# Input loads further ahead, and the first early job written after the eighth unit, in a gated scan with routed experts

## The chip, the core and the metric

The kernel runs on one core of one Trainium2 chip. The metric is the device time of an execution in microseconds (us). The engines are PE (TensorE, the matrix engine), DVE (VectorE), ACT (ScalarE), POOL (GpSimd) and SP (SyncE, which here only issues DMAs and reads registers). In the profile "PEld" is PE's loading of weights, "SPq" and "ACTq" are DMA issues by SP and ACT, and "Lnnn" is a line of the kernel.

## What is computed

A gated recurrence along the sequence feeds a two-level mixture of experts, in which every token goes to one of 16 experts:

```python
sig = 1.0 / (1.0 + np.exp(-f_logit))              # x, f_logit: 4 x 3648 x 256
f = lower_bound + (1.0 - lower_bound) * sig
h[t] = f[t] * h[t - 1] + (1 - f[t]) * x[t]        # for every batch row, start 0
# x is now h, 14592 tokens of 256
g = argmax(x @ w_group)                           # one of 4 groups
e = argmax(x @ w_expert[g])                       # one of 4 experts of the group
out[token] = softmax_g * softmax_e * (relu(x @ w1[g, e]) @ w2[g, e])   # 256 -> 1024 -> 256
```

## The kernel before, in words

**Units.** The 14592 tokens are worked through as 29 units of 512, numbered from 0 (so the eighth unit is unit 7). Unit u goes through these steps. `p1_load` (L167) brings 1 MB of inputs into one of four `zt` buffers; units up to 11 are loaded from SP's queue, later ones from ACT's. ACT computes the gate by Tanh and an affine step (`p1_tanh`, `p1_affine`, L185 to L203). DVE multiplies the input by the gate (L218 or L238) and runs one scan for each half of the 256 channels (`p1_tb`, L229). The scan of a unit starts from the last column of the unit before it. PE multiplies the result with the router's weights (`p1_router`, L275) and turns the answer over (`p1_logits`, L288). PE also turns the scan's result back into rows of tokens (`p1_back`, L256), which ACT copies out. For a group of one or two units (`GROUPS`) the routing follows: DVE finds the largest logits, PE counts the tokens of every expert (L380 to L383, "run-offs"), DVE computes each token's place, and POOL scatters the rows by indirect DMA into the lists `xs` in DRAM (L358), 128 rows at a time.

**Early jobs.** A list long enough is worked on before all units are done. `EARLY` gives 16 jobs as (unit, tiles of 128 tokens): jobs 0 and 1 at units 5 and 6, jobs 2 and 3 at unit 8, 4 and 5 at unit 10, and so on. At its unit, `pick` (L573) chooses on DVE the fullest list; SP reads the choice into a register (L589), and writes blank rows below the list's end (L592). Then come the weights of the job (`job_weights`, L841 to L849, asked for by `fetch_to`), the load of its rows `xr` (`job_rows`, L831), which waits for the scatters of all units ahead of its own, the transposes of these rows (`job_xt`, L912), and the two products with ReLU between (`m1_step`, `m2_step`). Jobs 0 and 1 are "raw": they multiply in fp32 (L943, L978) with no splitting of weights, with 22 matmuls for warming (`keep_warm`, L265) ahead of the transposes. The other jobs use split weights, three products each (L965 to L967, L995). After the units, 16 further jobs work off what is left of the lists.

**Order.** SP issues everything in the order in which the program is written. PE, DVE and ACT are held to the written order only inside the block at L1128 to L1131; what is written behind that block is placed by the scheduler, which may also move it ahead into gaps it sees. Inside the block stands all of the background program up to the mark of the first row load (`start_macro(0)` runs it up to `marks[5]`), and then job 0's weights and `job_xt`. The background program is a list of small functions made by `p1_thunks` (L404). Up to unit 9 (`FAST`) the part for unit u begins with the load of unit u + 2, then, by `ROWS_AT`, the row load of job 0 (at u = 6) or job 1 (at u = 7), and only then the gate of the next unit, the router of unit u - 1, the scans, the routing, and `pick`. `pick` ends with `fetch_to`, which asks for four pieces of weights. So before, job 0's transposes are written ahead of all the rest of unit 6. Behind the block, the jobs' products and the background program are interleaved by due times.

Of the kernel before, what the change touches and what calls it, by code (L numbers as in the profile page):

```python
# [36 lines left out]
O_BUFS = 5  # L37
X_BUFS = 4
AHEAD = 3
MT = -(-max(CAPS) // 128)  # L40
QUARTERS = (13, 14, 15)
ZX_SP = 12
# [3 lines left out]
def gated_scan_moe(ctx: ExitStack, tc, zx, lower, wroute, wexp, out, S):  # L46
# [118 lines left out]
    last_load = {}  # L165

    def p1_load(u):  # L167
        if u >= NU:
            return
        a, b = unit_range(u)  # L170
        w = b - a
        zt = p1.tile([P, 2, KD, UNIT], F32, name="zt", bufs=4)
        src = zx[u * P:(u + 1) * P, :].rearrange("p (s k w) -> p s k w", s=2, k=KD)
        if u == 0:
            for k in range(KD):
                for q in range(2):
                    nc.sync.dma_start(out=zt[:, q, k, 0:w], in_=src[:, q, k, 0:w])
        elif u == 1:
            for k in range(KD):
                nc.sync.dma_start(out=zt[:, :, k, 0:w], in_=src[:, :, k, 0:w])  # L180
        else:
            last_load[u] = (nc.sync if u < ZX_SP else nc.scalar).dma_start(out=zt[:, :, :, 0:w], in_=src[:, :, :, 0:w])
        units[u] = {"z": zt}
# [220 lines left out]
    def p1_thunks(us, groups, parts):  # L404
# [36 lines left out]
        def wave(u, n):  # L441
            while parts and n and parts[0][0] <= u:
                put(parts.pop(0)[1])
                n -= 1
# [13 lines left out]
        for u in us + [us[-1] + 1]:  # L458
            seq = []
            if u <= FAST:  # L460
                put(lambda u=u: p1_load(u + AHEAD - 1))
                for m in [m for m, v in ROWS_AT.items() if u == v]:
                    f = lambda m=m: early_rows(m)
                    f.mark = m
                    put(f)
                ending = u - 1 in ends
                if not ending:
                    put(lambda u=u: p1_ta(u + 1))
                if u > 0:
                    put(lambda u=u: p1_router(u - 1))  # L470
                    put(lambda u=u: logits(u - 1))
                    if u > 1:
                        put(lambda u=u: p1_gate(u))
                put(lambda u=u: p1_tb(u, 0))
                wave(u, 1)
                if ending:
                    bind, bound, (s1, f4x, s2, f3, f4, s6, f5, s7s) = routing(u - 1)
                    put(bind)
                    put(lambda u=u: p1_tanh(u + 1))
                    put(s1)  # L480
                    put(f4x)
                    if u > 1 and member[u - 2] == member[u - 1]:
                        back(u - 2)
                    put(s2)
                    put(f3)
                    put(f4)
                    wave(u, 1)
                    put(lambda u=u: p1_affine(u + 1))
                    back(u - 1)
                    put(bound)  # L490
                    put(s6)
                    put(f5)
                    for f in s7s:
                        put(f)
                    wave(u, 1)
                elif u > 7:
                    wave(u, 1)
                    back(u - 1)
                if u in cuts and u - 1 in ends:
                    put(lambda u=u: pick(u))  # L500
                put(lambda u=u: p1_tb(u, 1))
                wave(u, 1 if u < FAST else 99)
                if u == FAST:
                    f = lambda: None
                    f.mark = "begun"
                    put(f)
                    for v in [v for v in sorted(cuts) if v <= FAST and v not in ROWS_AT]:
                        f = lambda v=v: early_rows(v)
                        f.mark = v
                        put(f)  # L510
                continue
            if u in us:
                seq += [lambda u=u: (p1_load(u + AHEAD - 1), u + 1 in us and p1_ta(u + 1))]
            if u - 1 in us:
                seq += [lambda u=u: p1_back(u - 1, 0)]
            if u in us:
                seq += [lambda u=u: p1_tb(u, 0)]
            if u - 1 in us:
                seq += [lambda u=u: p1_router(u - 1)]
                seq += [lambda u=u: p1_back(u - 1, 1)]  # L520
            if u in us:
                seq += [lambda u=u: p1_tb(u, 1)]
            if u - 1 in us:
                seq += [lambda u=u: logits(u - 1)]
            for t in seq:
                put(t)
                slot += 1
                for _ in range(1):
                    if not hold:
                        break  # L530
                    f = hold.popleft()
                    if isinstance(f, tuple):
                        lagq.append((slot + LAG, f[1]))
                    else:
                        put(f)
                while lagq and lagq[0][0] <= slot:
                    put(lagq.popleft()[1])
            if u - 1 in ends:
                grp = ends[u - 1]
                T = sum(unit_range(v)[1] - unit_range(v)[0] for v in grp) // P  # L540
                G = {}

                def bind(G=G, first=grp[0]):
                    G.update(cur.pop("G"))
                    G["rows"] = group_rows.pop(first)
                if u <= 13:
                    s1, f4x, s2, f3, f4, s6, f5, s7s = route_thunks(G, T, True)
                    rs = [s1, s2, f3, f4x, None, f4, f5, s6] + s7s
                else:
                    rs = route_thunks(G, T)  # L550
                    rs[3:3] = [None] * 2
                put(bind)
                if u in cuts:
                    rs.append(lambda u=u: pick(u))
                    f = lambda u=u: early_rows(u)
                    f.mark = u
                    rs.append(("lag", f))
                hold.extend(rs)
# [14 lines left out]
    def pick(u):  # L573
# [24 lines left out]
        V.scalar_tensor_tensor(out=got, in0=pos, scalar=float(n * P), in1=eoff, op0=ALU.add, op1=ALU.subtract)  # L598
        V.tensor_tensor(out=got, in0=got, in1=sel, op=ALU.mult)
        V.tensor_tensor(out=taken, in0=taken, in1=got, op=ALU.add)  # L600
        fetch_to(pptr[0] + 4)

    asked = set()

# [255 lines left out]
    def job_xt(j, pi):  # L860
# [58 lines left out]
        else:  # L919
            hi = j.xh[ch][:, :, c0:c0 + rows]  # L920
            nc.scalar.copy(hi, tpv)
            nc.vector.tensor_tensor(out=j.xl[ch][:, :, c0:c0 + rows], in0=tpv, in1=hi, op=ALU.subtract)  # L922
        meta = mo.tile([P, 2, 2], I32, name="meta", bufs=16)
        tc.keep_in_program_order(nc.vector.tensor_copy(meta[:, 0:m], r[:, 0:m, D:D + 2]))
        if j.kind != "A":
# [201 lines left out]

    with tc.manual_schedule(engines={mybir.EngineType.PE, mybir.EngineType.DVE, mybir.EngineType.Activation}):  # L1128
        start_macro(len(PLAN))
        for t in prep_thunks(macros[len(PLAN)][0]):  # L1130
            t()  # L1131
    pending = None
# [92 lines left out]
```

## Time and profile before

| | us |
|---|---|
| median of 3 runs (lowest to highest) | 802.14 (800.18 to 803.07) |
| the profiled execution | 802.48 |
| its span in the trace | 800.7 |

Of the span PE is busy for 91%, DVE for 67%, ACT for 57% and POOL for 36%. The chip moves 152.02 MB by DMA, 189 GB/s over the span. The page shows the span in 40 slices of 20 us: in the first eight PE is busy for 2, 7, 2, 9, 8, 6, 8 and 5 tenths, and its granted clock is 9, 8, 6, 7, 9, 8, 9 and 7 tenths of full speed; after that PE stays at 9 and the clock too. A busy PE is no PE at its peak, since matmuls are pipelined and a lower clock stretches them, so a stretch is read by its idle time and its clock together.

### The profile page before, as it was taken

How to read it: one execution, taken by the hardware profiler on the slowest of the kernel's cores; microseconds unless marked ns; L12 is line 12 of the kernel's file. 1: busy time of each engine (PE TensorE's matmuls, PEld its weight loads, DVE VectorE, ACT ScalarE, POOL GpSimd, SP SyncE). 2: the span in 40 equal slices, each digit the busy share in tenths (PEclk: the TensorE clock that was granted, in tenths of full speed). 3: DMA queues.
4: the chain of work that ended last, by engine and by line, in shares of the span. 5: the costliest groups of instructions: out<-in, count | busy, mean ns of one | idle time of the engine just before them, and what ended most of it. 6: DMA issues, size and time to landing. Idle time of an engine off the chain costs nothing.

```text
span 800.7 us, 21431 instructions
## 1 busy us (share of the span) xinstructions
PE 725.3 (91%) x8131; PEld 641.8 (80%) x8131; DVE 535.2 (67%) x1140; ACT 453.4 (57%) x820; POOL 289.0 (36%) x272
## 2 busy tenths in 40 slices
PE   2729868599999999899999999999999999999995
PEld 1527646388888888799989989898999999889995
DVE  6945459589999999469645573645545656556651
ACT  6715557478788786445555554444454555546652
POOL 3641416435666556553112211222222223223222
PEclk9867989799999999999999999999999999999999
DMA  7672989968888865665788654344333555556530
GB/s 273 229 229 69 336 303 275 330 226 285 289 308 296 263 220 181 207 190 153 226 178 197 163 151 92 117 99 118 116 106 126 143 158 166 160 157 180 167 81 28
DMA packets 101977, 152.02 MB, mean 190 GB/s; under 512 B 60975, under 2 KB 71000, under 8 KB 98544
## 3 DMA queue, kind: packets, MB, share of 16 engines
q1 hardware_dynamic: 87328, 103.27, 45.8%
q0 software_dynamic: 11424, 30.02, 10.4%
q10 hardware_dynamic: 3120, 17.34, 5.9%
q8 instruction: 64, 1.05, 0.6%
q14 instruction: 41, 0.34, 0.2%
HBM read 112.66 MB, written 38.38 MB: 189 GB/s over the span
## 4 chain that ended last, share of the span: by engine, by line
PE 61%; DVE 12%; DMA 9%; issue 5%; ACT 4%; POOL 1%; SPq 1%; POOLq 0%; DVEq 0%; ACTq 0%
PE ps_m L995 29%; PE ps_m L965 6%; PE ps_m L966 6%; PE ps_m L967 6%; DVE wl L858 3%; PE ps_p L965 3%; PE ps_p L966 3%; PE ps_p L967 3%; DVE hl L971 2%; DMA zt<-in_zx_dram 2%; DVE h L229 2%; DMA xr<-xs 2%; DMA xs<-rows,posi 2%; DMA xs<-blank 1%; PE ps_p L256 1%
## 5 line engine op out<-in xcount | busy, mean ns | idle before, releaser
L995 PE MATMUL ps_m<-wh,hl 128*128 128x256 f16 (+4 forms) x1256 | 254.9, 251 | 0.1
L995 PE MATMUL ps_m<-wh,hh 128*128 128x256 f16 (+4 forms) x1256 | 254.7, 252 | 0.0
L995 PE MATMUL ps_m<-wl,hh 128*128 128x256 bf16 (+4 forms) x1256 | 254.6, 251 | 0.0
L995 PEld LDWEIGHTS <-hh 128*128 128x128 f16 (+4 forms) x2512 | 186.8, 99 | 22.0 <-issue 3.3
L966 PE MATMUL ps_m<-xl,wh 128*128 128x256 bf16 (+10 forms) x790 | 192.5, 257 | 5.9 <-DVE xl L922 3.2
L965 PE MATMUL ps_m<-xh,wh 128*128 128x256 f16 (+10 forms) x790 | 192.3, 257 | 3.2 <-DVE hl L971 2.7
L967 PE MATMUL ps_m<-xh,wl 128*128 128x256 f16 (+10 forms) x790 | 192.5, 257 | 0.0
L358 POOL DMA_INDIRECT xs<-rows,posi x114 | 138.4, 1214 | 128.2 <-issue 29.0
L858 DVE TENSOR_TENSOR wl<-st,wh 128x1024 bf16<-128x1024 f32 x120 | 144.6, 1217 | 52.9 <-ACT wh L857 52.7
L1008 POOL DMA_INDIRECT out_dram<-o,info x71 | 82.6, 1164 | 237.3 <-ACT o L1007 214.6
L971 DVE SCALAR_TENSOR_TENSOR hl<-ps_m,hh 128x512 bf16<-128x512 f32 (+9 forms) x169 | 112.4, 671 | 70.6 <-ACT hh L970 65.3
L970 ACT ACTIVATE hh<-ps_m 128x512 f16<-128x512 f32 (+9 forms) x169 | 99.3, 589 | 61.7 <-PE ps_m L967 58.6
L857 ACT CAST wh<-st 128x1024 f16<-128x1024 f32 x120 | 123.9, 1047 | 17.6 <-DMA st<-in_wexp_dram 7.7
L967 PEld LDWEIGHTS <-wl 128*128 128x128 bf16 x1088 | 107.2, 99 | 13.5 <-issue 6.2
L966 PEld LDWEIGHTS <-wh 128*128 128x128 f16 x1088 | 107.3, 99 | 11.3 <-issue 3.9
L965 PEld LDWEIGHTS <-wh 128*128 128x128 f16 x1088 | 107.3, 99 | 10.3 <-issue 1.4
L1008 POOL DMA_INDIRECT out_dram<-o,meta x57 | 63.1, 1107 | 138.8 <-ACT o L1007 116.7
L995 PEld LDWEIGHTS <-hl 128*128 128x128 bf16 (+4 forms) x1256 | 99.6, 99 | 10.1 <-issue 0.4
L1007 ACT ACTIVATE o<-ps_m,info 128x256 f32<-128x256 f32 (+3 forms) x71 | 31.6, 446 | 72.1 <-PE ps_m L995 64.2
L965 PE MATMUL ps_p<-xh,wh 128*128 128x256 f16 (+14 forms) x298 | 70.8, 252 | 0.0
L966 PE MATMUL ps_p<-xl,wh 128*128 128x256 bf16 (+14 forms) x298 | 70.7, 251 | 0.0
L967 PE MATMUL ps_p<-xh,wl 128*128 128x256 f16 (+14 forms) x298 | 70.6, 251 | 0.0
(181 smaller groups left out, 828.4 us busy)
## 6 DMA issues: line engine op xcount, KB each, us to landing
st<-in_wexp_dram SPq DMA_DIRECT2D x120, 512.0 KB, 6.3
zt<-in_zx_dram ACTq DMA_DIRECT2D x16, 1024.0 KB, 8.6
zt<-in_zx_dram SPq DMA_DIRECT2D x10, 1024.0 KB, 6.0
xs<-blank SPq DMA_DIRECT2D x28, 258.0 KB, 4.9
xr<-xs SPq DMA_DIRECT2D x14, 258.0 KB, 2.9
wh<-in_wexp_dram SPq DMA_DIRECT2D x8, 256.0 KB, 7.1
wl<-in_wexp_dram SPq DMA_DIRECT2D x8, 256.0 KB, 6.6
xs<-rows,posi POOLq DMA_INDIRECT x114, 7.3
```

The source lines that it names most:

```text
L229: nc.vector.tensor_tensor_scan(out=h[:, k, c0 - a:c1 - a], data0=ff[:, k, c0 - a:c1 - a], data1=uu[:, k, c0 - a:c1 - a], initial=init, op0 ...
L358: sc = nc.gpsimd.indirect_dma_start(out=xs_v[G["t0"] + t][:, :], out_offset=bass.IndirectOffsetOnAxis(ap=R["posi"][:, t:t + 1], axis=0), i ...
L857: nc.scalar.copy(j.wh[i], j.st[i])
L858: nc.vector.tensor_tensor(out=j.wl[i], in0=j.st[i], in1=j.wh[i], op=ALU.subtract)
L965: nc.tensor.matmul(po, w1_at(j.wh, k, c), xh[:, k], start=(k == 0), stop=False)
L966: nc.tensor.matmul(po, w1_at(j.wh, k, c), xl[:, k], start=False, stop=False)
L967: nc.tensor.matmul(po, w1_at(j.wl, k, c), xh[:, k], start=False, stop=(k == KD - 1))
L970: nc.scalar.activation(hi, pv, AF.Relu)
L971: nc.vector.scalar_tensor_tensor(out=j.hl[ch][:, cs[0]:cs[-1] + 1, 0:w], in0=pv, scalar=0.0, in1=hi, op0=ALU.max, op1=ALU.subtract)
L995: nc.tensor.matmul(pm[i * q:i * q + n, 0:dw], h[ch][:, c, ts], w2_at(w, c)[:, i * dw:(i + 1) * dw], start=(c == 0 and s == 0), stop=(c == ...
L1007: nc.scalar.activation(o[s, 0:dw], pm[s, 0:dw], AF.Copy, scale=lt.bitcast(F32)[s, r, 1:2])
L1008: nc.gpsimd.indirect_dma_start(out=out_v[out_n[0]].rearrange("n (g d) -> (n g) d", g=g), out_offset=bass.IndirectOffsetOnAxis(ap=lt[s, r, ...
```

## The change

Five edits. (1) Up to unit 9, the part for unit u now asks for the loads up to unit u + 3 (`FAR`), where it asked for unit u + 2; a unit that is loaded already is skipped. The number of buffers stays four. (2) The row loads of jobs 0 and 1 move from the start of the parts for units 6 and 7 to just ahead of the second scan there, behind `pick` of unit 6. (3) The weights that `pick` asked for at its end are now asked for behind these row loads (and behind `pick` elsewhere). (4) A new mark stands behind the scans of unit 7 (`BEGIN`), and the block with the written order runs the background program up to it before job 0's weights and transposes. (5) Raw jobs no longer copy token numbers and output weights out of the row tile, they read them from there.

```diff
--- before.py
+++ after.py
@@ -37,6 +37,8 @@
 O_BUFS = 5
 X_BUFS = 4
 AHEAD = 3
+FAR = 4
+BEGIN = 7
 MT = -(-max(CAPS) // 128)
 QUARTERS = (13, 14, 15)
 ZX_SP = 12
@@ -165,7 +167,7 @@
     last_load = {}
 
     def p1_load(u):
-        if u >= NU:
+        if u >= NU or u in units:
             return
         a, b = unit_range(u)
         w = b - a
@@ -458,11 +460,7 @@
         for u in us + [us[-1] + 1]:
             seq = []
             if u <= FAST:
-                put(lambda u=u: p1_load(u + AHEAD - 1))
-                for m in [m for m, v in ROWS_AT.items() if u == v]:
-                    f = lambda m=m: early_rows(m)
-                    f.mark = m
-                    put(f)
+                put(lambda u=u: [p1_load(v) for v in range(u + AHEAD - 1, u + FAR)])
                 ending = u - 1 in ends
                 if not ending:
                     put(lambda u=u: p1_ta(u + 1))
@@ -498,8 +496,18 @@
                     back(u - 1)
                 if u in cuts and u - 1 in ends:
                     put(lambda u=u: pick(u))
+                for m in [m for m, v in ROWS_AT.items() if u == v]:
+                    f = lambda m=m: early_rows(m)
+                    f.mark = m
+                    put(f)
+                if u in cuts and u - 1 in ends:
+                    put(lambda: fetch_to(pptr[0] + 4))
                 put(lambda u=u: p1_tb(u, 1))
                 wave(u, 1 if u < FAST else 99)
+                if u == BEGIN:
+                    f = lambda: None
+                    f.mark = "first"
+                    put(f)
                 if u == FAST:
                     f = lambda: None
                     f.mark = "begun"
@@ -551,7 +559,7 @@
                     rs[3:3] = [None] * 2
                 put(bind)
                 if u in cuts:
-                    rs.append(lambda u=u: pick(u))
+                    rs.append(lambda u=u: (pick(u), fetch_to(pptr[0] + 4)))
                     f = lambda u=u: early_rows(u)
                     f.mark = u
                     rs.append(("lag", f))
@@ -598,7 +606,6 @@
         V.scalar_tensor_tensor(out=got, in0=pos, scalar=float(n * P), in1=eoff, op0=ALU.add, op1=ALU.subtract)
         V.tensor_tensor(out=got, in0=got, in1=sel, op=ALU.mult)
         V.tensor_tensor(out=taken, in0=taken, in1=got, op=ALU.add)
-        fetch_to(pptr[0] + 4)
 
     asked = set()
 
@@ -920,6 +927,9 @@
             hi = j.xh[ch][:, :, c0:c0 + rows]
             nc.scalar.copy(hi, tpv)
             nc.vector.tensor_tensor(out=j.xl[ch][:, :, c0:c0 + rows], in0=tpv, in1=hi, op=ALU.subtract)
+        if j.raw:
+            j.meta.append(r[:, 0:m, D:D + 2])
+            return
         meta = mo.tile([P, 2, 2], I32, name="meta", bufs=16)
         tc.keep_in_program_order(nc.vector.tensor_copy(meta[:, 0:m], r[:, 0:m, D:D + 2]))
         if j.kind != "A":
@@ -1127,6 +1137,7 @@
 
     with tc.manual_schedule(engines={mybir.EngineType.PE, mybir.EngineType.DVE, mybir.EngineType.Activation}):
         start_macro(len(PLAN))
+        bg_to(marks["first"])
         for t in prep_thunks(macros[len(PLAN)][0]):
             t()
     pending = None
```

## Rows read from the trace of the kernel before

**Rows 1.** Page, first part: engine busy us, share of span, instructions.

```profile
PE 725.3 (91%) x8131; PEld 641.8 (80%) x8131; DVE 535.2 (67%) x1140; ACT 453.4 (57%) x820; POOL 289.0 (36%) x272
```

**Rows 2.** Stretches: length, busy of PE, PEld, DVE, ACT, POOL; clock, DMA share, GB/s.

```profile
45.60:60.70 15.10, 0.00 (x0) 0.03 (x1) 4.85 (x6) 0.48 (x1) 3.88 (x3) 0.63 0.87 270
60.70:70.00 9.30, 9.30 (x43) 6.43 (x43) 4.83 (x12) 4.55 (x11) 0.00 (x0) 0.50 0.00 0
85.70:88.60 2.90, 0.18 (x1) 0.01 (x1) 0.00 (x0) 0.43 (x1) 0.21 (x1) 1.00 0.98 362
105.10:112.30 7.20, 0.64 (x4) 0.25 (x2) 0.67 (x1) 4.23 (x6) 0.00 (x0) 0.91 0.81 303
144.30:153.50 9.20, 0.00 (x0) 0.00 (x0) 7.46 (x8) 6.51 (x10) 7.04 (x6) 0.73 1.03 402
200.00:315.00 115.00, 113.08 (x1168) 99.76 (x1165) 113.84 (x245) 91.41 (x173) 73.14 (x57) 1.00 0.80 268
350.00:792.00 442.00, 439.23 (x5437) 401.98 (x5436) 258.17 (x480) 226.87 (x383) 115.83 (x103) 1.00 0.54 146
```

**Rows 3.** Timeline, 59 to 90 us: start, us, engine, line, idle before and releaser.

```profile
60.22 1.06 ACT L192 ACTIVATE zt<-zt 128x1024 f32<-128x1024 f32 x1 [17.66 <-DMA zt<-in_zx_dram]
...
60.70 0.47 PE L912 MATMUL ps_p<-ident,xr 128*128 128x128 f32 x1 [15.12 <-DMA xr<-xs]
...
61.01 0.17 DVE L924 COPY meta<-xr 128x4 int32<-128x4 int32 x1 [10.53 <-DMA xr<-xs]
...
89.48 0.32 DVE L330 TENSOR_REDUCE sm<-ex 128x40 f32<-128x160 f32 x1 [10.92 <-ACT ex L388]
```

**Rows 4.** Timeline of SP's DMA issues, 0 to 100 us.

```profile
4.66 24.35 SPq L182 DMA_DIRECT2D zt<-in_zx_dram  x6
...
50.96 0.34 SPq L182 DMA_DIRECT2D zt<-in_zx_dram  x1
...
73.19 0.36 SPq L592 DMA_DIRECT2D xs<-blank  x1
...
79.33 0.34 SPq L182 DMA_DIRECT2D zt<-in_zx_dram  x1
...
92.84 0.79 SPq L182 DMA_DIRECT2D zt<-in_zx_dram  x1
```

**Rows 5.** Stretches, columns as in rows 2.

```profile
33.80:45.45 11.65, 9.57 (x109) 8.15 (x107) 10.76 (x31) 7.94 (x18) 9.07 (x9) 0.77 0.36 129
60.70:72.00 11.30, 11.30 (x79) 7.72 (x79) 6.68 (x24) 5.72 (x15) 0.12 (x1) 0.59 0.00 0
72.00:153.50 81.50, 56.88 (x397) 44.40 (x393) 55.36 (x121) 50.39 (x95) 37.57 (x32) 0.91 0.91 306
```

**Rows 6.** Chain of waits in order of time: start, us, what.

```profile
49.12 7.22 DMA xs<-rows,posi
56.58 3.98 DMA xr<-xs
...
133.03 8.52 DMA xs<-rows,posi
141.56 11.86 DMA xr<-xs
```

**Rows 7.** Groups on PE, 60.7 to 79.4: count, busy us, mean ns, idle before.

```profile
L256 PE MATMUL ps_p<-ident,h 128*128 128x128 f32 x24 | 4.5, 328 | 0.0
L275 PE MATMUL ps_p<-h,wr 128*32 128x128 f32 x64 | 3.6, 314 | 0.0
...
L380 PE MATMUL ps_p<-runoff,row 1*128 1x80 f32 (+1 forms) x4 | 1.2, 395 | 0.0
L288 PE MATMUL ps_p<-ident,rs 128*128 128x128 f32 x3 | 1.0, 332 | 0.0
```

**Rows 8.** Timeline of DVE, 30 to 52 us: second scan of unit 4; of unit 7.

```profile
33.78 1.27 DVE L229 TENSOR_TENSOR_SCAN h<-zt,h 128x512 f32<-128x512 f32 x1
...
49.41 1.07 DVE L229 TENSOR_TENSOR_SCAN h<-zt 128x448 f32<-128x448 f32 x1
```

## The prediction

> **What bounds the kernel now.** I read the engine shares first. PE (TensorE) is busy for 725.3 us of 800.7 [rows 1], so the end moves only if PE waits less or does its early work at the higher clock. The table of stretches says where it waits. From 350 to 792 us PE is busy for 439.23 of 442 us, and from 200 to 315 us for 113.08 of 115, while DVE (VectorE) is busy for 113.84 there [rows 2]. Neither stretch has anything to give, and both need rows and units delivered earlier if they are to end earlier. The idle time lies ahead of them: 15.1 us (45.6 to 60.7), 2.7 us (85.7 to 88.6), 6.6 us (105.1 to 112.3) and 9.2 us (144.3 to 153.5) [rows 2]. Then the waits and the chain say who ended these. At 60.70 PE had waited 15.12 us for the rows of job 0. ACT had then waited 17.66 us for the input of unit 8. DVE's next long stop, 10.92 us at 89.48, ends with an exponential on ACT, which itself stood behind the Tanh of unit 9 [rows 3]. That input was asked for only at 79.33, because SP issues in written order and the load stood behind job 1's choice, blank rows and eight weight loads, which began at 73.19 [rows 4]. The choice was late because it needs the routing of unit 5, whose PE work stood behind job 0's transposes. So one blocked instruction at 45.6 made three later waits. While it lasted, transfers dried up too: from 60.7 to 72.0 the DMA share is 0.00, and from 72.0 to 153.5 it is 0.91 [rows 5]. The second half of the early stage is paced by transfers whose first 11.3 us were given away.
>
> **Part by part.**
>
> *Job 0's program after unit 7.* In the block with a written order, units 6 and 7 now come before job 0's 22 warming matmuls and four transposes. The rows of job 0 come no sooner: the last scatter they wait for starts at 49.12 and takes 7.22 us, the load 3.98 us [rows 6], so about 60.6. But in 45.6 to 60.7 PE ran nothing, and it can now do what it did for units 5 and 6 behind the rows. The groups after 60.7 give 3.6 us for the routers of four units (half, 1.8), 4.5 us for the back transposes of three (one of them falls before the mark, 1.5), 1.0 for the logits transposes of three (two, 0.7) and 1.2 for the run-off products of two routings (one, 0.6; with the counts behind it I take 1.0) [rows 7]. Sum 5.0 us off the path. The cover is DVE's: it must do unit 5's routing, the second choice and the scans of 6 and 7 by then. The scans of 6 and 7 ended by 50.8 [rows 8], and DVE was busy only 4.85 of the 15.1 us, so 10.2 us are free; the 9.3 us after 60.7, which hold unit 5's routing with a gate and a scan, took 4.83 us [rows 2]. With two waits for the run-off copy of some 1.5 us I put the mark at 56 to 61 us. If it slips past 60.6, each us costs one us, up to the 5.0 gained.
>
> *Loads three units ahead.* Loads up to 7 already go out the moment their buffer is free (six issues over 24.35 us [rows 4]); nothing is gained there. Load 8 needs the buffer of unit 4, whose second scan starts at 33.78 [rows 8]; it is now written ahead of the first choice and goes out near 35.1 in place of 50.96, into a stretch with a DMA share of 0.36 [rows 5]. Load 9 comes behind job 0's weights, at about 51 in place of 79.33. Load 10 comes behind job 1's weights, at about 62. Load 11 waits for unit 7's scans and stands behind job 1's rows: about 65 in place of 92.84 [rows 4]. So the ACT waits of 17.66 us and the DVE wait of 10.92 us [rows 3] should go, and with them the PE stops of 2.7 and 6.6 us [rows 2], since the second is ReLUs queued on ACT behind the input of units 11 and 12 and job 2's late rows. The new waits: on SP, loads 9 to 11 wait for scans of unit 5, 6 and 7, with row loads and weights queued behind; by the times above those scans are over when SP arrives, cost 0, at worst one pair of scans, about 2.5 us [rows 8]. Load 12 goes out from ACT right behind unit 8's scans. The trace of before has no such wait on ACT; between 0 and a gate with two scans (about 4 us) I take 1, because ACT's copies for routing stand ahead of it.
>
> *The second choice ahead of the first row load.* On SP the value load, 1 blank and then job 0's row load; only after that the eight weight loads of job 1 (some 0.7 us apiece, between the blank at 73.19 and the load at 79.33 [rows 4]). Job 0's row load is held by the scatters until 56.3 [rows 6] anyway, so a choice made by about 54 costs nothing; each us that the choice is later than 56.3 delays job 0's rows by as much. Before, the row load waited for no choice of unit 6. This and the mark have the same cover, and the same price.
>
> *Raw jobs take their offsets and weights out of the row tile.* Two DVE copies go (0.17 us each, nothing on the sum); the 10.53 us that DVE stood at the first one [rows 3] goes with the reordering. In return the row buffers of jobs 0 and 1 are held until their outputs are written. There are six; jobs 2 and 3 take one each, job 4 two, so job 5 would be the first to meet them, long after. Cost 0.
>
> **The sum.** From PE: 5.0 + 2.7 + 6.6 = 14.3 us, less 1 for load 12. From transfers, independently: the empty 11.3 us are refilled (job 1's weights, loads 10 and 11, unit 5's scatters), up to 3.5 us more from moving load 8 (1 MB at the 306 GB/s of the busy stretch) [rows 5]. Both describe the same shift of the early stage and are not added. I take 12 us. The 9.2 us before 153.5 stay: their chain is scatter 8.52, then row load 11.86 us [rows 6], and nothing in the change shortens it; it only begins sooner. The clock I leave out: PE ran 60.7 to 70.0 at a granted 0.50 (1.2 GHz) [rows 2] after 15 idle us, which cost 4.65 us; with PE partly occupied before, some may come back. The profiled execution took 802.5 us, hence 790.5; the median of the runs is 0.3 below it, hence 790. After 160 us PE and DVE are both full, so the shift is handed on whole.
>
> **Rivals.** *Only the reordering counts (about 797).* If SP's queue keeps loads 9 to 11 about where they were, the 5.0 us of PE work remain: 802.1 - 5. For it: SP must still wait for the choice and for scatters of unit 5. Against it: load 9 stands ahead of both.
>
> *Given back at the row loads (about 802).* From 72 us on transfers run at 0.91 [rows 5]. If jobs 2 to 5 get their rows when they do now because the scatters of units 6 to 9 are no earlier, PE, having done jobs 0 and 1 sooner, waits longer at 105 and 144. For it: 402 GB/s just before 153.5 [rows 2], at which nothing more fits. Against it: those scatters followed on DVE stops that should vanish.
>
> *Slower: the early loads crowd job 0's rows (about 807).* Job 0's scatters and row load are alone on the path. A row load took 3.98 us here and 11.86 us at 141.56, where much else was in flight; the scatters before them 7.22 and 8.52 us [rows 6]. With loads 8 to 10 and two jobs' weights beside them, job 0 could get its rows 7.9 + 1.3 = 9.2 us later, 69.8. PE has 5.0 us of earlier work to set against it, so the kernel loses 4.2 us if the later waits return too: 802.5 + 4.2 = 806.7. It decides from a landing later than 65.6. Against it: in 45.6 to 60.7 the share was already 0.87 [rows 2], and load 8 has left that stretch.
>
> The Trainium skill (DMA: Bandwidth & Descriptors, section Queues, rings and completion order) speaks for this rival: every one of the sixteen engines takes its queue rows in turn, packet by packet, so loads from SP and scatters from POOL slow each other whoever issued first. By that rule alone, a scatter and row load each sharing evenly would double, 11.2 us more, which would make it about 809; the row at 133.03, 8.52 us in a crowded stretch, does not bear out a doubling of the scatter.
>
> **How the numbers follow.** Forecast (a gain of 8 to 20 us): 0.55. Only the reordering: 0.15. Given back: 0.15. Slower: 0.15. Less than 0.5% (4 us) can't be told from no change by a measurement of this kernel. So faster 0.70, same 0.15, slower 0.15. For the range: the low end adds to 14.3 the 4.65 us of clock and about half of the 9.2, 24 us, so 778; the high end takes in the reordering alone and nearly all of the case given back, 803, and leaves out the slower one.
>
> **What would show it.** Right: PE busy for some 5 us between 45 and 60; load 8 near 35 and load 9 near 51; no DVE stop of 10 us near 80 to 90; no hole in the DMA share at 60 to 72; row loads of jobs 2 and 3 asked for before 100. Wrong: job 0's rows landing after 65, the mark after 61, ACT standing at an input load, or the stops before 112 and 153 grown by what the first one lost.

## The result, and the profile after

The changed kernel takes 782.77 us, the median of four runs (779.46 to 783.77); the kernel before, run beside it, takes 801.92 (800.18 to 803.07). The ratio is 0.9756, with a 95% interval of 0.9722 to 0.9790, a gain of 19.15 us. The forecast was 790 with a range of 778 to 803, so sign and range held, and the gain was larger than the 12 us forecast. The profiled execution took 783.77 us with a span of 782.0.

First part of the changed kernel's page (busy us, share of the span, instructions):

```profile
span 782.0 us, 21416 instructions
...
PE 721.4 (92%) x8131; PEld 639.9 (82%) x8131; DVE 534.6 (68%) x1138; ACT 452.5 (58%) x820; POOL 293.5 (38%) x272
```

Against [rows 1], PE runs the same 8131 matmuls in 3.9 us less, and its idle time fell from 800.7 - 725.3 = 75.4 to 782.0 - 721.4 = 60.6 us, 14.8 less. The two add up to the 18.7 us between the spans. Where the idle time went is read from the same stretches of both kernels. Before (length, then busy PE, PEld, DVE, ACT, POOL, then clock, DMA share, GB/s):

```profile
0.00:40.00 40.00, 20.82 (x171) 14.34 (x172) 32.37 (x98) 28.64 (x55) 20.77 (x44) 0.95 0.71 251
40.00:160.00 120.00, 80.17 (x579) 62.24 (x577) 73.21 (x169) 59.68 (x118) 45.96 (x39) 0.82 0.79 257
160.00:200.00 40.00, 40.00 (x466) 35.51 (x463) 36.18 (x75) 31.12 (x60) 16.71 (x15) 1.00 0.75 256
200.00:350.00 150.00, 144.66 (x1487) 127.54 (x1484) 135.30 (x320) 106.59 (x204) 88.77 (x72) 1.00 0.73 241
```

The changed kernel:

```profile
0.00:40.00 40.00, 19.21 (x170) 13.12 (x171) 32.06 (x97) 26.99 (x53) 20.72 (x43) 0.89 0.75 259
40.00:160.00 120.00, 94.70 (x781) 77.61 (x780) 86.61 (x190) 73.33 (x145) 48.78 (x43) 0.85 0.87 285
160.00:200.00 40.00, 39.48 (x448) 35.12 (x447) 39.48 (x88) 32.36 (x62) 23.99 (x23) 1.00 0.80 275
200.00:350.00 150.00, 145.85 (x1448) 127.73 (x1446) 128.31 (x303) 101.04 (x192) 92.38 (x71) 0.99 0.73 237
```

From 40 to 160 us PE's idle time falls from 39.8 to 25.3 us, 14.5 of the 14.8. In the other three stretches it moves by at most 1.6 us (up before 40 us, down after 200), so the shift is handed on and not given back. Beside it the share of the DMA engines rises from 0.79 to 0.87.

The stretches of [rows 2] up to 153.5 us, in the changed kernel, with those between them:

```profile
45.60:60.70 15.10, 9.55 (x103) 8.27 (x99) 13.74 (x34) 7.37 (x16) 8.20 (x8) 0.80 0.92 288
60.70:70.00 9.30, 6.07 (x33) 4.22 (x34) 1.53 (x2) 3.77 (x7) 0.00 (x0) 0.63 0.67 198
70.00:85.70 15.70, 14.80 (x118) 12.50 (x117) 10.38 (x29) 10.61 (x25) 6.98 (x7) 1.00 0.99 310
85.70:88.60 2.90, 2.90 (x17) 2.40 (x15) 1.29 (x2) 1.78 (x7) 2.51 (x2) 1.00 0.95 313
88.60:105.10 16.50, 10.23 (x53) 8.30 (x53) 11.13 (x14) 10.23 (x17) 0.00 (x0) 0.72 0.81 247
105.10:112.30 7.20, 6.99 (x60) 5.17 (x60) 3.77 (x18) 3.04 (x6) 0.00 (x0) 0.93 0.69 262
...
144.30:153.50 9.20, 9.02 (x116) 7.94 (x115) 6.83 (x12) 6.41 (x11) 2.08 (x2) 1.00 1.00 288
```

PE works for 9.55 of the 15.1 us in which it stood [rows 2], and DVE for 13.74 in place of 4.85. Much of PE's part is no work of the units: summed by instruction, 66 warming matmuls take 6.8 us of this stretch, which before the change ran from 40.86 us on, ahead of the stop, and the units' own matmuls take 4.0 us. The hole in the transfers from 60.7 us on is filled: 0.67 and then 0.99, where [rows 5] had 0.00 up to 72. From 60.7 to 70 the granted clock is 0.63 where it was 0.50 [rows 2]. But a stretch cut at the same microseconds holds other work now, and the idle time at 105 and 144 us may only have moved. That is told by the stops themselves. PE in the changed kernel (start, us, operation; in brackets the idle time ahead of it and what ended it):

```profile
45.08 0.65 PE L277 MATMUL ps_p<-h,wr 128*32 128x128 f32 x8 [3.10 <-DVE h L231]
...
53.99 0.42 PE L277 MATMUL ps_p<-h,wr 128*32 128x128 f32 x8 [3.12 <-DVE h L231]
...
63.93 0.49 PE L919 MATMUL ps_p<-ident,xr 128*128 128x128 f32 x1 [4.72 <-DMA xr<-xs]
...
74.75 0.22 PE L383 MATMUL ps_p<-oh16f,upto 128*128 128x128 bf16 x1 [0.90 <-DVE oh16f L371]
...
100.03 1.12 PE L919 MATMUL ps_p<-ident,xr 128*128 128x128 f32 x4 [6.27 <-DMA xr<-xs]
...
136.77 1.76 PE L919 MATMUL ps_p<-ident,xr 128*128 128x128 f32 x6 [5.83 <-DMA xr<-xs]
```

The later stops of the kernel before:

```profile
88.62 0.86 PE L912 MATMUL ps_p<-ident,xr 128*128 128x128 f32 x4 [2.73 <-DMA xr<-xs]
...
112.27 0.46 PE L912 MATMUL ps_p<-ident,xr 128*128 128x128 f32 x1 [6.56 <-DMA xr<-xs]
...
137.69 0.27 PE L966 MATMUL ps_m<-xl,wh 128*128 128x256 bf16 x1 [3.23 <-DVE xl L922]
153.56 1.80 PE L912 MATMUL ps_p<-ident,xr 128*128 128x128 f32 x6 [9.78 <-DMA xr<-xs]
```

In part it had only moved: the stop of job 0's rows shrank, but two waits for scans of 3.1 us stand ahead of it; the stop of 2.73 us for job 1's rows is gone; the stop of jobs 2 and 3 came 12 us sooner and is nearly as long as before; that of jobs 4 and 5 lost some 4 us. SP's DMA issues of the changed kernel show what was asked for when:

```profile
4.74 30.94 SPq L184 DMA_DIRECT2D zt<-in_zx_dram  x7
44.00 0.37 SPq L600 DMA_DIRECT2D xs<-blank  x1
...
49.43 0.44 SPq L184 DMA_DIRECT2D zt<-in_zx_dram  x1
52.55 0.36 SPq L600 DMA_DIRECT2D xs<-blank  x1
61.76 1.31 SPq L838 DMA_DIRECT2D xr<-xs  x2
...
67.48 0.54 SPq L184 DMA_DIRECT2D zt<-in_zx_dram  x1
69.36 0.89 SPq L838 DMA_DIRECT2D xr<-xs  x2
70.37 0.55 SPq L184 DMA_DIRECT2D zt<-in_zx_dram  x1
...
97.21 2.92 SPq L838 DMA_DIRECT2D xr<-xs  x4
```

Load 8 is the last of the seven issues that end by 35.7; load 9 goes out at 49.43 and load 11 at 70.37, where [rows 4] had 79.33 and 92.84. Job 0's row load stands at 61.76. The scatters alone would have let it go at 56.3 [rows 6]. What it waited for, from SP's waits between 50 and 66 us (us in total, times, longest):

```profile
SPq L838 <- DMA xs<-blank: 5.4, 1, 5.4
SPq L597 <- DVE sel L603: 2.2, 1, 2.2
SPq L838 <- DMA xs<-rows,posi: 2.0, 1, 2.0
```

After 2.0 us for the scatters it stood 5.4 us for the landing of the blank rows of job 1, which the second choice had put into the queue at 52.55. The prediction did not see that wait.

ACT's stops at inputs fell from 17.66, 3.50, 6.41 and 0.66 us to two, of 5.28 us (below) and 0.54 us:

```profile
60.76 1.06 ACT L194 ACTIVATE zt<-zt 128x1024 f32<-128x1024 f32 x1 [5.28 <-DMA zt<-in_zx_dram]
```

### The profile page after: what moved, and what is told of

It reads as the page before. It is cut to its first block, busy times and chain, and to the rows that moved or that the text cites. A ratio compares the mean times of both kernels' runs of the same rounds, so it can differ in the third digit from the quotient of the medians.

```text
span 782.0 us, 21416 instructions
## 1 busy us (share of the span) xinstructions
PE 721.4 (92%) x8131; PEld 639.9 (82%) x8131; DVE 534.6 (68%) x1138; ACT 452.5 (58%) x820; POOL 293.5 (38%) x272
## 4 chain that ended last, share of the span: by engine, by line
PE 55%; issue 11%; DVE 10%; DMA 6%; POOL 3%; ACT 1%; SPq 1%; POOLq 0%; DVEq 0%; ACTq 0%
PE ps_m L1005 27%; PE ps_m L975 6%; PE ps_m L976 6%; PE ps_m L977 6%; PE ps_p L975 3%; PE ps_p L977 3%; PE ps_p L976 3%; DVE h L231 2%; DMA xs<-rows,posi 2%; DVE wl L865 2%; DVE hl L981 2%; POOL out_dram L1018 2%; DMA st<-in_wexp_dram 1%; DMA xr<-xs 1%; DVE zt L220 1%
## 5 line engine op out<-in xcount | busy, mean ns | idle before, releaser
L360 POOL DMA_INDIRECT xs<-rows,posi x114 | 144.2, 1265 | 124.9 <-issue 50.1
L1018 POOL DMA_INDIRECT out_dram<-o,info x71 | 82.3, 1159 | 234.9 <-ACT o L1017 213.4
L1018 POOL DMA_INDIRECT out_dram<-o,meta x53 | 57.3, 1080 | 120.3 <-ACT o L1017 93.3
```

Source lines behind the costliest of these rows:

```text
L360: sc = nc.gpsimd.indirect_dma_start(out=xs_v[G["t0"] + t][:, :], out_offset=bass.IndirectOffsetOnAxis(ap=R["posi"][:, t:t + 1], axis=0), i ...
L1018: nc.gpsimd.indirect_dma_start(out=out_v[out_n[0]].rearrange("n (g d) -> (n g) d", g=g), out_offset=bass.IndirectOffsetOnAxis(ap=lt[s, r, ...
```

## The experiments

The theory at the outset was the prediction's: the later stops shrink because loads 8 to 11 are asked for sooner, and PE does unit 5's and 6's work while it waits for job 0's rows; the early second choice and the raw copies cost nothing. The rivals were that one of the two does it alone, that the early choice costs, and that the copies matter. Later ones were that the two edits need each other, that the row load stands for the blank rows, that the warming matmuls, which now run nearer to the rows, hold the clock up, and that units, not jobs, pace the stage. The quoted texts name them by letters.

Three sets were run, each on one chip with the kernel before beside it. On chips A and B every kernel took 5 to 6% longer than on chip C and in the result above, so only ratios to the kernel before of the same set are compared. The changed kernel itself was run beside others on chip B only, so a comparison with it across chips is weaker than one within a chip.

| run | what it is | chip | median us | before us | ratio (95%) |
|---|---|---|---|---|---|
| x1_far3 | changed, loads two units ahead | A | 837.82 | 850.09 | 0.9862 (0.9798 to 0.9927) |
| x2_nomark | changed, no mark | A | 826.34 | 850.09 | 0.9738 (0.9672 to 0.9803) |
| x3_order | changed, row loads ahead of the choice | A | 818.07 | 850.09 | 0.9643 (0.9584 to 0.9701) |
| x4_copy | changed, raw copies kept | A | 819.79 | 850.09 | 0.9683 (0.9623 to 0.9744) |
| y_changed | the changed kernel | B | 822.93 | 847.42 | 0.9725 (0.9693 to 0.9757) |
| y_order | the same program as x3_order | B | 816.33 | 847.42 | 0.9647 (0.9612 to 0.9682) |
| b1_far | before, loads three units ahead | B | 843.10 | 847.42 | 0.9949 (0.9926 to 0.9972) |
| b2_mark | before, the mark alone | B | 836.18 | 847.42 | 0.9874 (0.9841 to 0.9907) |
| z1_both | before, loads and mark, nothing else | C | 777.47 | 799.46 | 0.9737 (0.9678 to 0.9796) |
| z2_blank | changed, job 1's blank rows behind job 0's row load | C | 778.31 | 799.46 | 0.9728 (0.9687 to 0.9768) |
| z3_nowarm | changed, raw jobs' warming left out | C | 783.07 | 799.46 | 0.9793 (0.9759 to 0.9826) |
| z4_begin8 | y_order, mark behind unit 8 | C | 778.66 | 799.46 | 0.9736 (0.9701 to 0.9770) |

### Loads only two units ahead (x1_far3)

```diff
-FAR = 4
+FAR = 3
```

> The changed kernel with loads asked for two units ahead again; order, mark and raw jobs as changed. Theory A (the working on record: the loads remove the waits of ACT and DVE at 80 to 90 and with them the PE stops of 2.7 and 6.6 us): about 9 us slower than the changed kernel, 792. Theory B (all of the gain is the loads): 802. Theory C (the early stage is paced by transfers and the written order alone decides, so a load asked for sooner lands no sooner when it counts): 783, no difference.

0.9862, where the changed kernel on chip B has 0.9725 (and x2_nomark and x4_copy, on the same chip A, 0.9738 and 0.9683). ACT stood at inputs for 8.45 and 9.63 us, and jobs 2 and 3 had their row load at 105.44 (102.56 in y_changed). The third unit ahead is worth about 1.4% once the rest is in place.

### No mark (x2_nomark)

```diff
         start_macro(len(PLAN))
-        bg_to(marks["first"])
```

> The changed kernel without the mark: job 0's program follows its row load directly, behind the second choice of unit 6 but ahead of unit 6's second scan and all of unit 7. Theory A: routing of unit 5 is already ahead of it, so most of the 5.0 us of PE work stays in front; unit 6's router and logits (about 1 us) and the scans of 6 and 7 fall behind the transposes; 784 to 787. Theory B (loads): 783. Theory C (the written order decides): 790 or more.

0.9738, not told apart from the changed kernel's 0.9725 on chip B. The likely reason, read from the program: with the row load of job 0 written behind the second choice, running the background program up to that row load already writes most of the part for unit 6 ahead of job 0's transposes. In the trace the products of unit 5's routing run at 58.40, job 0's transposes at 69.48. So the early choice of edit 2 is a second way to nearly the same order.

### Row loads back ahead of the choice (x3_order, y_order)

The loop `for m in ... early_rows(m)` moves back behind the loads, to the start of the parts for units 6 and 7; both runs are the same program.

```diff
                 put(lambda u=u: [p1_load(v) for v in range(u + AHEAD - 1, u + FAR)])
+                for m in [m for m, v in ROWS_AT.items() if u == v]:
+                    f = lambda m=m: early_rows(m)
+                    f.mark = m
+                    put(f)
...
                     put(lambda u=u: pick(u))
-                for m in [m for m, v in ROWS_AT.items() if u == v]:
-                    f = lambda m=m: early_rows(m)
-                    f.mark = m
-                    put(f)
```

> The changed kernel with the row loads of jobs 0 and 1 back at the start of the parts for units 6 and 7, ahead of the second choice. In the trace of the changed kernel job 0's row load left at 61.8 behind the landing of job 1's blank rows (5.4 us of waiting) and PE waited 4.72 us for it. Theory D (that wait is on the path): row load at about 56.5, PE's 4.72 us go, 778 to 780. Theory E (the early choice brings job 1's weights and the next load sooner, and that pays for the wait): 785 to 788, with load 10 later than 67.5. Neither: 783.

> The changed kernel with the row loads of jobs 0 and 1 ahead of the second choice, beside the changed kernel on the same chip. Theory D (job 0's row load no longer waits 5.4 us for the landing of job 1's blank rows, PE starts job 0 that much sooner): 0.004 to 0.006 below the changed kernel's ratio. Theory E (the early choice pays for the wait): 0.003 to 0.006 above it.

0.9643 on chip A, 0.9647 on chip B. On chip B the intervals of y_order (up to 0.9682) and of the changed kernel (from 0.9693) do not touch: there, loading the rows behind the choice costs 6.6 us. SP's issue of job 0's rows in y_order and then in y_changed:

```profile
62.16 1.02 SPq L838 DMA_DIRECT2D xr<-xs  x2
```

```profile
69.22 1.31 SPq L838 DMA_DIRECT2D xr<-xs  x2
```

7.1 us apart, and SP's waits in y_changed show 5.9 us at this load for the blank rows. PE begins job 0's transposes 3.3 us apart, at 68.20 and 71.46, since the later load lands sooner. But the wait itself is not what the 6.6 us consist of. PE's idle time over the span is the same, 814.8 - 732.6 = 82.2 us in y_order and 821.9 - 739.6 = 82.3 in y_changed; what differs is its busy time for the same 8131 matmuls, by 7.0 us, at a mean granted clock of 0.966 and 0.957 in the profiled runs. How the order brings that about is not shown.

### Raw copies kept (x4_copy)

```diff
-        if j.raw:
-            j.meta.append(r[:, 0:m, D:D + 2])
-            return
```

> The changed kernel with the two copies of token numbers and weights put back for raw jobs. My working gave this edit 0: 783. Rival: the copy stands in the written order on DVE behind the row load and stops DVE as before (10.5 us then), now with less behind it since units 6 and 7 are done: 3 to 5 us slower, 786 to 788. Rival the other way: the row buffers come free sooner and the row load that waited 0.3 us for an output at 131 gains that: 782.5, not to be told from no change.

0.9683 (0.9623 to 0.9744) overlaps the changed kernel's 0.9725 (0.9693 to 0.9757). The fifth edit is worth nothing that these runs tell apart.

### The changed kernel on chip B (y_changed)

> The changed kernel itself, as the measure for the others of this call, given as a ratio to the kernel before on the same chip. 0.976 if the ratio is the same on every chip.

0.9725, in line with the result. It is the measure for the next two and for y_order.

### Only the loads (b1_far) and only the mark (b2_mark), in the kernel before

```diff
+FAR = 4
...
-        if u >= NU:
+        if u >= NU or u in units:
...
-                put(lambda u=u: p1_load(u + AHEAD - 1))
+                put(lambda u=u: [p1_load(v) for v in range(u + AHEAD - 1, u + FAR)])
```

```diff
+BEGIN = 7
...
+                if u == BEGIN:
+                    f = lambda: None
+                    f.mark = "first"
+                    put(f)
...
         start_macro(len(PLAN))
+        bg_to(marks["first"])
```

> The kernel before with the loads asked for three units ahead and nothing else. Theory A (loads and order act on different waits, 5.0 and 9.3 us): ratio 0.988. Theory B (the gain is the loads): 0.976. Theory C (the written order decides): 1.000. Theory F (the two need each other: job 0's blocked transposes still hold up the routing of unit 5, and so SP's choice and the loads behind it): 0.990 to 1.000, with load 8 at 35 but load 9 still behind 73.

> The kernel before with the mark alone: job 0's program written behind unit 7's scans; the loads two units ahead, the row loads ahead of the second choice. Theory A: 0.994. Theory B: 1.000. Theory C: 0.976 to 0.982. Theory F: 0.990 to 1.000, with the waits of ACT for inputs still there.

Alone they give 0.5% and 1.3%; the product of the two ratios is 0.982. Together, in y_order (which has the fifth edit too), the ratio is 0.9647: another 1.8%, some 15 us of 847, belongs to neither alone. SP's queue in b1_far shows why:

```profile
59.08 0.38 SPq L183 DMA_DIRECT2D zt<-in_zx_dram  x1
61.42 0.90 SPq L832 DMA_DIRECT2D xr<-xs  x2
79.78 0.36 SPq L593 DMA_DIRECT2D xs<-blank  x1
...
86.14 1.16 SPq L183 DMA_DIRECT2D zt<-in_zx_dram  x1
```

Load 9 goes out at 59.08, but load 10 stands behind the second choice, which is late because job 0's transposes still come ahead of unit 5's work on PE: blank rows at 79.78, load 10 at 86.14. In y_order, with the mark, load 10 goes out at 73.51. ACT's input stops in b1_far remain 13.56 and 6.96 us. In b2_mark the choice is earlier but the loads are asked for one unit at a time, and ACT stands 8.62 and 9.78 us. With the mark that stop reaches job 0: the part for unit 7 is now written ahead of its transposes, in it ACT takes the gate of unit 8, whose input is late, ahead of a copy for the logits, and PE stands for that copy.

```profile
67.75 1.06 ACT L193 ACTIVATE zt<-zt 128x1024 f32<-128x1024 f32 x1 [8.62 <-DMA zt<-in_zx_dram]
```

```profile
70.56 0.47 PE L289 MATMUL ps_p<-ident,rs 128*128 128x128 f32 x1 [7.93 <-ACT rs L281]
```

PE's idle time over the span is 98.8 us in b1_far and 96.5 in b2_mark, and 82.2 in y_order. In these runs an earlier request helped little where something late was queued ahead of it, and an earlier place in the order helped little where its input was late. How the gain is shared was measured on chip B alone.

### Only the loads and the mark, on a chip like that of the result (z1_both)

Relative to y_order:

```diff
-        if j.raw:
-            j.meta.append(r[:, 0:m, D:D + 2])
-            return
```

> The kernel before with both the loads three units ahead and the mark, and nothing else (row loads ahead of the second choice, raw jobs with their copies). Alone they measured 0.995 and 0.987. Theory A (they act on separate waits): 0.982. Theory F (each lifts what holds the other up: the loads stand in SP's queue behind a choice that waits for a routing that the blocked transposes hold): as low as the changed kernel with the row loads ahead, 0.965; then raw jobs' copies are worth nothing. 0.968 to 0.972 would give the copies 3 to 6 us.

777.47 us, 0.9737. As far as these runs can tell, two edits of the five give the whole gain. Both forecasts, 0.982 and 0.965, lie outside the interval; they were worked out from ratios of the other chips, and how much the two edits help each other on chip C was not measured. PE's stop for job 0's rows is 2.10 us, and the row load goes out at 56.39 where the changed kernel has 61.76:

```profile
56.39 0.90 SPq L838 DMA_DIRECT2D xr<-xs  x2
```

```profile
61.88 0.39 PE L919 MATMUL ps_p<-ident,xr 128*128 128x128 f32 x1 [2.10 <-DMA xr<-xs]
```

PE begins job 0 2.05 us sooner than in the changed kernel, and its idle time from 40 to 160 us is 21.0 us where the changed kernel has 25.3. The ratio lies 0.2% below the changed kernel's 0.9756, well within both intervals. A version that beats the changed kernel is shown on chip B (y_order), not on chip C.

### Job 1's blank rows behind job 0's row load (z2_blank)

```diff
+                if u == 6:
+                    put(late_blank)
...
             picked.add(j.idx)
+            if u == 6:
+                continue
```

`late_blank` issues the DMA that `pick` left out.

> The changed kernel, the second choice still ahead of job 0's row load, but job 1's blank rows written behind that row load. Theory D (the row load waits for the landing of the blank rows, not for the choice): row load some 6 us sooner than in the changed kernel, ratio 0.965 as with the row loads moved ahead. Theory D2 (it is the choice itself, or the place of the row load behind it): 0.972 as the changed kernel.

SP's waits from 40 to 66 us in z2_blank:

```profile
SPq L599 <- DVE sel L607: 9.8, 2, 6.9
SPq L618 <- DMA xr<-xs: 5.5, 1, 5.5
SPq L847 <- DMA xs<-rows,posi: 2.1, 1, 2.1
```

The choice stands ahead of the row load as in the changed kernel, but the row load waits for scatters only and goes out at 55.85; now the blank DMA waits 5.5 us for the row load. So it is the transfer of the blank rows into the lists, not the choice, that held job 0's rows. Both go to lists in `xs`, and the wait runs whichever comes second. The forecast that went with this, 0.965, was not met: the time, 0.9728, is not told apart from 0.9756, and on chip C what this wait costs is below what the runs resolve.

### Without the warming matmuls (z3_nowarm)

```diff
         if j.raw:
-            keep_warm(bank("m2"), 22)
             j.xh[ch] = mo.tile([P, 2 * P], F32, name="xh", bufs=X_BUFS)
```

> The changed kernel without the 22 warming matmuls of each raw job. On their own they took 4.2 us for 44 on PE in a stretch where PE waited anyway. Theory G (the clock that the changed kernel got back hangs on them): PE busy some 3 us longer at the lower clock, ratio 0.975 to 0.977. Theory H (the clock came back because the stop ahead of job 0 is shorter): 0.9725, PE busy shorter by the 4.2 us and the clock as low in 60 to 67 as with them.

In the changed kernel's own profile the 44 warming matmuls of jobs 0 and 1 take 4.20 us from 55.01 on. Stretches of z3_nowarm:

```profile
45.60:60.70 15.10, 6.00 (x55) 4.35 (x55) 13.75 (x34) 7.71 (x17) 8.04 (x8) 0.61 0.87 288
60.70:70.00 9.30, 6.29 (x29) 3.82 (x29) 1.38 (x2) 3.17 (x6) 0.00 (x0) 0.54 0.64 195
```

The granted clock is 0.61 and 0.54 where the changed kernel has 0.80 and 0.63, and PE's busy time over the span is 719.5 us, where 721.4 less 4.2 would be 717.2: the other matmuls took 2.3 us longer. That looks like the theory that warming near the rows buys back clock, but the other runs of chip C do not bear it out. With the warming in the same place, z2_blank has 0.63 and 0.66 in these two stretches and z1_both 0.66 and 0.82, and PE's busy time is 727.3 and 720.7 us; less 4.2 that is 723.1 and 716.5, and 719.5 lies between them. The ratio, 0.9793 (0.9759 to 0.9826), overlaps the changed kernel's (0.9722 to 0.9790), and the profiled spans are 781.6 and 782.0. What the warming is worth, in clock or in time, stays open.

### The mark behind unit 8 (z4_begin8)

Relative to y_order:

```diff
-BEGIN = 7
+BEGIN = 8
```

> The changed kernel with the row loads ahead of the second choice (0.965) and the mark one unit later, behind unit 8's scans. Theory A (a mark that falls behind the landing of job 0's rows costs a microsecond each): unit 8 brings the routing of units 6 and 7, some 5 to 6 us of DVE, behind which job 0 now stands, so 0.970 to 0.972. Rival (the units pace the stage, jobs 0 and 1 fill gaps anyway): 0.963 to 0.966.

0.9736, the same as z1_both. Job 0's transposes begin at 66.50 in place of 61.88 (z1_both), 4.6 us later. The row loads of jobs 2 and 3 go out at 87.94, 4.8 us sooner than in z1_both, and PE begins those rows at 97.07 without a stop, where z1_both stands 4.08 us and begins at 96.66; z4_begin8 stands 5.65 us for job 1's rows instead. PE's idle time from 40 to 160 us is 22.4 against 21.0 us, and the medians lie 1.2 us apart. This fits the rival, by which the units pace this stage and jobs 0 and 1 fill its gaps. The price that the prediction put on a late mark, one us for each us behind job 0's rows, would be 4.6 us here and is not seen; the intervals, some 3 to 5 us to either side, are too wide to exclude it by the times alone.

## Why the prediction was right, and where it was not

**What bounds the kernel: right in the main.** PE's busy time moved by 3.9 us, its idle time by 14.8, and 14.5 of these lie between 40 and 160 us. After 200 us the shift is handed on; the rival "given back at the row loads" falls, since the rows of jobs 2 and 3 were asked for at 97.21 in place of 109.90. One reading was off: transfers did not dry up "while it lasted". In the 15.1 us of the stop the DMA share was 0.87 [rows 2], and the empty stretch came behind it [rows 5].

**The sum: right in total, wrong in its terms.** PE's stops by event, from the timelines of both kernels (small ones included):

| stop | before | after | change | forecast |
|---|---|---|---|---|
| up to job 0's rows | 15.1 | 11.9 | -3.2 | -5.0 |
| job 1's rows [rows 2: 85.7 to 88.6] | 2.7 | 0 | -2.7 | -2.7 |
| small stops up to jobs 2 and 3 | 1.2 | 0.9 | -0.3 | not counted |
| rows of jobs 2 and 3 | 6.8 | 6.3 | -0.5 | -6.6 |
| small stops up to jobs 4 and 5 | 4.2 | 0.2 | -4.0 | not counted |
| rows of jobs 4 and 5 | 9.8 | 5.8 | -4.0 | 0 ("stay") |
| sum | 39.8 | 25.1 | -14.7 | -14.3 |

The first term had its work right and its end wrong: counted from the start, PE was busy for 31.3 us by job 0's transposes, where before it had been for 26.4, so 4.9 us more of it came ahead of them; but the rows came at 63.93 and not at the 60.6 that the prediction took over from the kernel before. The step "the second is ReLUs queued on ACT behind the input of units 11 and 12" failed: ACT's input stops mostly went, and the stop of 6.6 us stayed, because it ends with a row load that follows scatters and moves with them. The trace of before said so already: that stop ends with the DMA of the rows (the line at 112.27 above). The step "the 9.2 us before 153.5 stay" failed the other way: the row load there lands in 5.45 us (chain of the changed kernel, next line) where it took 11.86 [rows 6].

```profile
131.18 5.45 DMA xr<-xs
```

And the 4.2 us of small stops on split rows and ReLUs, of which the longest was 3.23 us, had not been read at all. So errors of both signs cancelled: 7.9 us of the forecast did not come, and 8.3 us came that were not forecast. That the sum held is luck in this part. The second working, from the transfers (the 11.3 us hole of [rows 5]), named no stop and came to the same total. It has support in the rows of the two kernels above: up to 160 us the changed kernel moved (259 - 251) x 40 + (285 - 257) x 120 = 3680 KB more, an estimate of 12 us at the 306 GB/s of [rows 5]. That transfers, and not the order on PE, set the total is not shown by it.

**Forecast of 12, measured 19.15.** Of the 7.15 us between them, 3.9 are PE's busy time, which the sum did not have: the same 8131 matmuls took 3.9 us less. The prediction had kept up to 4.65 us for the clock in its range, but that these 3.9 us are the clock is not shown. The mean granted clock of the two profiled runs is 0.966 and 0.967, and z2_blank, on chip C and at 0.966 too, was busy for 727.3 us. 1.3 are the step from 13.3 down to the 12 taken, for which no row stood. 1.0 is the wait set down for load 12: ACT issued it at 76.60, where it had been 100.17, and no stop of PE answers to it. Another 0.5 is idle time beyond the 14.3 (14.8 over the whole span). What is left is the step from the profiled run to the median.

**Loads three units ahead: right on when, wrong on how the gain is shared.** Loads 8 to 11 went out near 35, 49, 67 and 70, forecast 35, 51, 62 and 65; DVE's stop of 10.92 us went and ACT's fell from 28.2 to 5.8 us. One of the prediction's signs of being wrong did come: ACT stood 5.28 us at load 9. And splitting the gain into 5.0 for the order and 9.3 for the loads was wrong: alone the loads give 0.5%, the order 1.3%, together 3.5% on chip B (b1_far, b2_mark, y_order). The rival "only the reordering" falls, since loads 9 to 11 went out sooner; its price of 5 us for the order was low too, as the order alone gave 847.42 - 836.18 = 11.2 us on chip B.

**The second choice ahead of the row load: the step failed.** It was priced at 0 for a choice made by 54. The choice was made by then, with its blank rows out at 52.55. What was missed is the DMA behind the choice: the row load stood 5.4 us for its landing, and went out at 61.76, not 56.4. On chip B that edit costs 0.8%; on chip C it is below what the runs resolve. The later load took 2.2 us from issue to PE in the changed kernel's own profile and in y_changed, where the one ahead of the choice took 5.5 (z1_both) and 6.0 (y_order), so PE began job 0 only 2.05 and 3.3 us later. Why the cost shows on one chip and not on the other stays open.

**The mark and its cover: the cover held, the price was not seen.** DVE was busy for 13.74 of the 15.1 us and unit 7's scans ended at 58.7, inside the forecast 56 to 61. No cost of a later mark is seen (z4_begin8), and with edit 2 no gain of the mark itself is (x2_nomark).

**Raw jobs: 0, as far as the runs tell.** The row buffers were not met as late as the prediction had it: the row load at 131.18, for jobs 4 and 5, went out when a raw job's output had been written, after SP had stood 0.3 us for that. x4_copy does not tell the edit from nothing.

**The slower rival: its mechanism is there, below its point of decision.** Job 0's rows reached PE at 63.93, short of the 65.6 from which it would decide. Load 9 took 11.3 us from its issue at 49.43 to ACT's start on it, at a DMA share of 0.92. Job 0's row load took, from issue to PE, 2.2 us at a share of 0.32 (the changed kernel), 4.1 at 0.77 (before), 5.5 at 0.71 (z1_both) and 6.0 at 0.86 (y_order). The rule of even sharing that the prediction named from the Trainium skill (DMA: Bandwidth & Descriptors, Queues, rings and completion order) agrees with these rows in direction; the doubling that it would give over the 4.1 us of before is not seen in them.

## What to carry to other kernels

Where one queue issues in written order, price asking for a load earlier and freeing what stands ahead of it in the queue together, and not as a sum. A step moved in a queue brings its DMAs along, so for each ask which later transfer waits for its landing. And when a stop on the critical engine ends with a transfer, expect it to move with its cause rather than vanish, and count all small stops of the stretch before writing any large one off.

## What the runs showed of the hardware

The same program took different times in sets on different chips: the changed kernel 782.77 us beside a before of 801.92, and on chip B 822.93 beside 847.42, with the same number of instructions (21416). The trace of chip B shows stops that wait for nothing the profile shows ("issue") or for nothing that it can name ("remote"). One of PE and one of ACT in y_changed:

```profile
44.13 0.48 PE L290 MATMUL ps_p<-ident,rs 128*128 128x128 f32 x1 [7.07 <-issue]
```

```profile
43.81 0.27 ACT L282 COPY rs<-ps_p 128x128 f32<-128x128 f32 x1 [7.17 <-remote]
```

Other runs on A and B have PE's stop at the same instruction, of 4.82 to 7.01 us (x1_far3, b1_far, y_order); the trace of the result has none there. DVE in y_changed, at the step that splits the ReLU's result:

```profile
DVE hl L981 <- issue: 41.4, 14, 5.4
```

41.4 us in 14 stops that wait for nothing the profile shows; in the changed kernel's own profile this group waits only for ACT. PE's busy time is longer as well, 739.6 us against 721.4. What holds the engines there was not settled; the ratios of the same program on A and B (0.9643 and 0.9647) agree closely all the same.

The granted clock also differs between programs that do nearly the same on PE: from 45.6 to 60.7 us it is 0.80 in the changed kernel's profile and 0.66 and 0.63 in z1_both and z2_blank, which run the warming matmuls in the same place. The cause was not looked for.
